# A fused attention and two-layer MLP kernel: two half-bank output accumulators, freer input products, casts on either of two engines, and a re-planned order

## Chip, cores and metric

One NeuronCore of a Trainium2 chip runs the whole program in a single launch. The metric is the device time of that launch in microseconds; the time before is the median of three runs.

## The reference

Attention with a learned position bias, then two MLP layers over its 2304 output rows (4 batches of 576 positions, 8 heads of 64). All results are float32; the weights of the MLP layers come as float64.

```python
scores = q @ k.T / 8 + bias          # bias[i, j, h] = relu(x @ w1 + b1) @ w2, x = log1p|i-j| / log1p(max(i,1))
attn = softmax(scores)
x = concat_heads(attn @ v)           # (2304, 512)
h = x @ w_in                         # 512 -> 2048
x = (s * relu(h)**2 + b) @ w_out     # 2048 -> 512: the first layer
h = x @ w_in2
out = (h - tanh(h)) @ w_out2         # the second layer
```

## The kernel before

**Engines.** PE multiplies, DVE and ACT do the elementwise work and read PSUM, POOL does some subtractions in SBUF, and SP issues every DMA. All products are made from float16 pairs: a value is split into a high half (a cast) and a low half (value minus high half), and a product is high x high, high x low and low x high, three matmuls.

**Order.** Nothing is issued in the order of the code. Each piece of work is a `Task` with its dependencies, a cost for each engine that could do it, a priority, and the buffers that it takes. `Schedule.forward` (L266) plays the program through with these costs and emits each task where it was played, so that every engine's queue is a fixed list in the built program. Buffers are counted by rings (L560): a task that takes a buffer of a ring waits until the users of the oldest one are done. Tables at the top of the file set the plan: `COST` and `XFER` correct the costs by kind of task, `ENGINE` pins single tasks to an engine, `SHIFT` moves the priority of single tasks. A transfer is modelled by the issue time on SP, a bus that takes one transfer after the other, and a delay to landing.

**Stages.** (a) The bias tables, the attention's scales and the first layer's weight conversion; (b) attention in 144 units (`qk` L1003, row minimum L1035, exponential L1045, high half L1055 or L1057, low half on POOL L1064, a transposing DMA L1070, `pv` L1083), and beside it the first layer for the blocks that are complete; (c) behind the last unit the rest of the first layer, while the second layer's weights are loaded (only the attention's buffers have room for them: the `turn` task), converted from float64 by three DVE operations (L1194, L1197, L1200), normed (L1723), split (L582, L585) and combined (L1775); (d) the second layer, whose products are saved from eight to seven by Strassen's scheme (`in_product` L1964, `out_product` L2092).

**The first layer** (`moe1_in` L1474, `moe1_tasks` L1530) works on nine blocks of 256 rows. A block has sixteen input steps of twelve 128x256 matmuls (L1499), two of which fill one PSUM bank `ph`. For each pair ACT takes the relu into `r` (L1512), ACT squares it (L1517), DVE casts it to the high half in `hr` (L1522), and POOL subtracts for the low half (L1526). Rings allow two `ph` banks and two `r` buffers. `hr` exists once: the casts of a block wait until the output steps of the block before are done. Then come four output columns of four steps each (L1568), each step again twelve 128x256 matmuls, gathered over its four steps in `po`. `po` is one PSUM bank in two halves that are used in turn (`po_tile`), but the ring `o` has a single place: the first matmul of a column waits until the column before has been read out by ACT (L1587) or DVE (L1582), two or three instructions by the batch borders in the block. Two lines tie the order on PE:

```python
last = t_poq.get(n - 1, [])[-1:]      # L1540: input steps come after the output steps of block n-1
("h", 2), ("o", 1), ("r", 2),         # L562: rings and their places
```

The second layer also takes a place of ring `o`: the last accumulator of `out_product` is the whole `po` bank.

Of the kernel before, what the change touches and what calls it, by code (L numbers as in the profile page):

```python
# [8 lines left out]
F32 = mybir.dt.float32  # L9
# [21 lines left out]
AHEAD = 5.97  # L31
# [4 lines left out]
    "u.ttr@dve": 0.8262, "f.hi@dve": 1.1781, "x.scale@dve": 1.04, "x.hi@dve": 1.03, "u.hi@dve": 0.9737,  # L36
    "s.in_done@dve": 1.78, "scan.add@dve": 0.73, "f.lambda@dve": 0.884, "s.out_done@dve": 1.2, "u.lo@pool":
    1.03, "f.lo@pool": 0.9595, "bias.lambda@pool": 0.992, "u.qk@pe": 0.885, "u.pv@pe": 0.97, "u.tr@sp": 1.17,
    "x.lambda@sp": 1.07, "q.fn@sp": 1.36, "J.c@dve": 1.13, "J.fn@dve": 1.12, "L.lambda@dve": 1.07,
# [3 lines left out]
    0.857, "v.hi@dve": 1.34, "v.lambda@dve": 0.968, "w.lambda@dve": 0.965, "f.lo@act": 0.95, "f.lo@dve": 0.95,  # L43
    "f.hi@act": 0.99, "f.hi@pool": 0.99, "u.hi@pool": 0.91, "u.ex@dve": 0.8, "u.ex@pool": 0.8, "u.ttr@act":
    0.81, "u.ttr@pool": 0.81,
}
XFER = {
    "bias.fn": (0.927, 0.75), "f.fn": (1.133, 0.55), "k.fn": (1.0815, 0.8), "q.fn": (0.8755, 1.15), "scan.fn":
    (0.9579, 0.8), "u.fn": (1.236, 1.41), "u.tr": (0.9991, 1.54), "v.fn": (1.0712, 1.3), "w.fn": (1.03, 0.87),
    "x.fn": (1.236, 0.55), "x.lambda": (0.721, 3.44), "L.fn": (0.9991, 0.9), "J.fn": (0.721, 0.3), "X.fn":  # L50
    (1.854, 0.4), "o.fn": (0.8858, 0.0),
}
# [331 lines left out]
def tile_kernel(  # L384
# [14 lines left out]
    nc = tc.nc  # L399
# [1074 lines left out]
    def moe1_in(n, o, w, ms, ready, prev_evac, prev, last, t_rlo):  # L1474
# [13 lines left out]
        for fp in range(KF // 2):  # L1488
# [32 lines left out]
            def hi(_, rh=rh, r=r):  # L1521
                nc.vector.tensor_copy(out=rh[:, :, 0, :], in_=r.tile)  # L1522
# [730 lines left out]
```

## Time and profile before

| | |
|---|---|
| median of three runs | 1078.2 us (1075.01 to 1080.54) |
| the profiled execution's own time | 1072.9 us |
| its span, first to last instruction | 1071.1 us |
| PE busy | 962.1 us, 90% of the span |
| DVE busy | 898.9 us, 84% |
| ACT busy | 664.7 us, 62% |
| POOL busy | 350.7 us, 33% |
| last instruction of attention on DVE starts | 572.67 us |

The profile shows one execution. Busy time is the union of an engine's instructions in a stretch; a matmul's row shows its whole passage, some 0.22 to 0.28 us, while matmuls follow each other much closer, so that PE's pace is read from many rows and not from the mean of one. "A <- B" in a list of waits is idle time of A's engine that ended when B was done.

### The profile page before, as it was taken

The numbers are of one execution on the slowest core, as the hardware profiler recorded it, in microseconds if no ns is written. First come the engines' busy times: TensorE is split into PE (matmuls) and PEld (weight loads), VectorE is DVE, ScalarE is ACT, GpSimd is POOL, SyncE is SP. The second block draws the span as 40 slices with busy tenths as digits, with TensorE's granted clock in tenths as the row PEclk, the third lists the DMA queues.
The fourth block names the chain that finished last, engine by engine and source line by source line (L and its number), as shares of the span: only waits on it lengthen the run. The fifth ranks groups of instructions, "written<-read, shape, count | busy, mean of one in ns | idle before, by whom it ended". The sixth has DMA issues, their size and how long they took to land.

```text
span 1071.1 us, 32375 instructions
## 1 busy us (share of the span) xinstructions
PE 962.1 (90%) x13370; PEld 820.5 (77%) x13370; DVE 898.9 (84%) x1914; ACT 664.7 (62%) x1279; POOL 350.7 (33%) x371
## 2 busy tenths in 40 slices
PE   5565658999998899999999898987999999999998
PEld 2222236778787688787888787877999999999998
DVE  6899899767668777786773989889999999999876
ACT  6788879868766576777753575656645543344433
POOL 6034355646456376585762342300000000000000
PEclk9667669999999999999999999999999999999999
DMA  9969987999999999989996705310101100100001
GB/s 340 360 153 250 296 230 149 208 211 255 244 181 234 201 171 199 206 172 194 173 171 167 300 10 173 105 36 16 32 23 41 42 22 31 32 22 22 21 2 41
DMA packets 261444, 153.66 MB, mean 143 GB/s; under 512 B 197680, under 2 KB 229552, under 8 KB 261296
## 3 DMA queue, kind: packets, MB, share of 16 engines
q1 hardware_dynamic: 261296, 151.59, 58.8%
q8 instruction: 104, 1.70, 0.7%
q14 instruction: 44, 0.36, 0.1%
HBM read 84.03 MB, written 20.33 MB: 97 GB/s over the span
## 4 chain that ended last, share of the span: by engine, by line
PE 55%; DVE 21%; DMA 12%; ACT 4%; issue 4%; POOL 3%; SPq 1%; DVEq 0%; ACTq 0%; POOLq 0%
PE acc L2092 13%; PE ph L1499 9%; PE pa L1964 8%; PE po L1568 8%; DMA et<-hl 8%; PE pb L1964 6%; PE sp L1003 3%; DVE w1big L585 3%; DVE sp L1035 2%; PE po L2092 2%; PE xp L1083 2%; POOL hr L692 1%; ACT e L1045 1%; DMA w1big<-in_wout 1%; DMA bi<-btd 1%
## 5 line engine op out<-in xcount | busy, mean ns | idle before, releaser
L1064 POOL TENSOR_TENSOR hl<-e,hl 128x64 f16<-128x64 f32 (+1 forms) x288 | 231.9, 828 | 221.0 <-ACT hl L1057 93.6
L1568 PE MATMUL po<-hr,w1big 128*128 128x256 f16 x1728 | 205.8, 275 | 13.2 <-ACT x L1587 8.6
L1568 PEld LDWEIGHTS <-w1big 128*128 128x128 f16 x1728 | 166.7, 99 | 39.2 <-issue 18.8
L1499 PEld LDWEIGHTS <-w1big 128*128 128x128 f16 x1728 | 165.2, 98 | 26.7 <-issue 8.0
L1964 PEld LDWEIGHTS <-w2big 128*128 128x128 f16 x3024 | 174.1, 98 | 4.2 <-issue 4.2
L2092 PEld LDWEIGHTS <-w1big 128*128 128x128 f16 x3024 | 172.8, 98 | 2.1 <-issue 2.1
L1045 ACT ACTIVATE e<-sp,mx 128x576 f32<-128x576 f32 x144 | 105.7, 734 | 53.7 <-DVE mx L1039 39.2
L1526 POOL TENSOR_TENSOR hr<-r,hr 128x512 f16<-128x512 f32 x72 | 100.4, 1396 | 115.8 <-DVE hr L1522 104.6
L1035 DVE CUSTOM_DVE_ANT_0 sp<-sp,bi 128x576 f32<-128x576 f32 x144 | 109.6, 761 | 31.9 <-PE sp L1003 26.5
L1499 PE MATMUL ph<-xt_own,w1big 128*128 128x256 f16 x960 | 112.5, 273 | 1.0 <-ACT r L1512 0.6
L1003 PE MATMUL sp<-ks,qs 64*128 64x288 f16 (+1 forms) x960 | 82.8, 298 | 13.9 <-ACT e L1045 11.3
L1083 PEld LDWEIGHTS <-et 128*128 128x128 f16 (+1 forms) x1440 | 54.9, 103 | 49.8 <-DMA et<-hl 26.6
L1499 PE MATMUL ph<-w1big 128*128 128x256 f16 x768 | 89.7, 275 | 1.6 <-ACT r L1512 1.2
L1083 PE MATMUL xp<-vp,et 128*128 128x64 f16 (+1 forms) x1440 | 65.5, 198 | 23.5 <-DMA et<-hl 17.8
L1057 ACT ACTIVATE hl<-e 128x576 f16<-128x576 f32 x100 | 67.5, 680 | 24.4 <-DMA et<-hl 21.1
L2092 PE MATMUL acc<-hr,w1big 128*128 128x128 f16 x1296 | 80.2, 219 | 1.8 <-DVE hr L585 1.2
L1003 PEld LDWEIGHTS <-qs 64*128 64x128 f16 (+1 forms) x960 | 46.3, 99 | 43.0 <-issue 32.8
L2092 PE MATMUL acc<-w2big,w1big 128*128 128x128 f16 x1296 | 79.1, 219 | 0.0
L1964 PE MATMUL pa<-w1big,w2big 128*128 128x128 f16 x960 | 61.2, 221 | 4.0 <-ACT w1big L1983 4.0
L1512 ACT ACTIVATE r<-ph 128x512 f32<-128x512 f32 x72 | 42.6, 592 | 31.0 <-PE ph L1499 22.4
L1522 DVE CAST hr<-r 128x512 f16<-128x512 f32 x72 | 42.2, 588 | 17.6 <-ACT r L1517 16.0
L1517 ACT ACTIVATE r<-r,sq 128x512 f32<-128x512 f32 x72 | 51.8, 720 | 1.5
(225 smaller groups left out, 1686.1 us busy)
## 6 DMA issues: line engine op xcount, KB each, us to landing
bi<-btd SPq DMA_DIRECT2D x64, 288.0 KB, 4.1
w1big<-in_wout SPq DMA_DIRECT2D x12, 1024.0 KB, 5.8
btd<-et SPq DMA_DIRECT2D x36, 295.5 KB, 4.4
w1big<-in_win SPq DMA_DIRECT2D x8, 1024.0 KB, 8.0
w2big<-in_win SPq DMA_DIRECT2D x8, 1024.0 KB, 12.8
x2d<-x SPq DMA_DIRECT2D x36, 128.0 KB, 2.2
w1big<-x2d SPq DMA_DIRECT2D x36, 128.0 KB, 2.4
outT<-xt_own SPq DMA_DIRECT2D x18, 256.0 KB, 2.2
```

The costliest lines, as they stand in the source:

```text
L1003: nc.tensor.matmul(out=out, lhsT=qs.tile[64 * h:64 * h + 64, sq, p * r:p * r + r], rhs=ks.tile[64 * h:64 * h + 64, sk, half * HS:(half + 1 ...
L1035: nc.vector.tensor_tensor_reduce(out=st, in0=st, in1=bi.tile.rearrange("p (a b) -> p a b", a=2), scale=-1.0 / KAP, scalar=3.0e38, op0=ALU. ...
L1045: nc.scalar.activation(out=put(e, row_tile("e")).rearrange("p (a b) -> p a b", a=2), in_=sp.tile[:, :, 0:HS], func=AF.Exp, scale=-1.0, bia ...
L1057: nc.scalar.activation(out=h[:, 0:S], in_=e.tile, func=AF.Copy)
L1064: (nc.gpsimd if eng == POOL else nc.vector).tensor_tensor(out=hl.tile[:, o:o + m], in0=e.tile[:, c:c + m], in1=hl.tile[:, c:c + m], op=ALU ...
L1083: nc.tensor.matmul(out=xp[r0:r0 + r, o:o + 64], lhsT=et.tile[:, n, r0:r0 + r], rhs=vp.tile[:, 0, n % 5, 64 * h:64 * h + 64], start=n == 0, ...
L1499: nc.tensor.matmul(out=ph.tile[:, fi, :], lhsT=win_ap(1, sw, m, f), rhs=xa(sx, m), start=m == 0 and j == 0, stop=m == KM - 1 and j == 2,)
L1517: nc.scalar.activation(out=r.tile, in_=r.tile, func=AF.Square, scale=sq[:, fp // 4:fp // 4 + 1])
L1526: (nc.gpsimd if e == POOL else nc.vector).tensor_tensor(out=rh[:, :, 1, :], in0=r.tile, in1=rh[:, :, 0, :], op=ALU.subtract)
L1568: nc.tensor.matmul(out=po.tile[:, :NB1], lhsT=wout_ap(1, sw, f, c), rhs=rhl[f // 8][:, f % 8, sr, :], start=f == 0 and j == 0, stop=f == K ...
L1964: nc.tensor.matmul(out=bank.tile[:, f * HT:(f + 1) * HT], lhsT=w[:, sw, m, f * 128:(f + 1) * 128], rhs=xs[:, sx, m], start=p in (1, 2, 5) ...
L2092: nc.tensor.matmul(out=bank.tile[:, o + c * HT:o + (c + 1) * HT], lhsT=w[:, sw, f, c * 128:(c + 1) * 128], rhs=g[:, sx, f], start=new and ...
```

## The change

1. Ring `o` has two places, so a column may start in the other half of the `po` bank while the half before is read out. Where the second layer uses `po` as a whole it takes both places (`more`).
2. The input steps of block n come after the input steps of the block before, no longer after its output steps.
3. The high-half cast in the first layer may run on ACT as well as on DVE. The table pins the casts of blocks 0, 1, 3, 4, 5, 7 and 8 to ACT, those of block 2 to DVE, and leaves block 6 open; the program has 57 on ACT and 15 on DVE.
4. The small tile `nm` has nine buffers in place of one.
5. The planner's model: SP is held longer by an issue when the modelled bus has a backlog (`BACK`), and COST, XFER, HOP, AHEAD, ENGINE and SHIFT have new numbers. With them the order of all engines is new. The instructions are the same apart from the engine that runs them: against before, DVE loses 57 casts L1522 and 32 scaled copies L580 and gains 14 casts L1055, 7 read-outs L1582 and 7 relus L692; ACT has the converse.

```diff
-    HOP = dict(pe=0.33, act=0.07, dve=0.16, pool=0.41, turn=0.0)
+    HOP = dict(pe=0.25, act=-0.04, dve=0.1, pool=0.61, turn=0.0)
+    BACK, BACK_MIN, BACK_HOLD = 0.5, 1.6, 1.1
...
-                free[eng] = at + cost[0]
+                hold = cost[0]
+                if eng == "sp" and hold > self.BACK_HOLD and bus - at > self.BACK_MIN:
+                    hold += self.BACK * (bus - at - self.BACK_MIN)
+                free[eng] = at + hold
...
-        ("h", 2), ("o", 1), ("r", 2), ("xt", 4), ("x2", 2), ("xf", 2), ("xh", 2), ("sum", 4),
+        ("h", 2), ("o", 2), ("r", 2), ("xt", 4), ("x2", 2), ("xf", 2), ("xh", 2), ("sum", 4),
...
-            nm = c2_t[n, o, "m"] = sm.tile([128, 1], F32, tag="nm", name="nm", bufs=1)
+            nm = c2_t[n, o, "m"] = sm.tile([128, 1], F32, tag="nm", name="nm", bufs=9)
...
-            def hi(_, rh=rh, r=r):
-                nc.vector.tensor_copy(out=rh[:, :, 0, :], in_=r.tile)
-            th = sc.add({DVE: 0.07 + 0.6e-3 * 2 * w}, hi, [ts] + prev, ready - 400, [], [r])
+            def hi(e, rh=rh, r=r):
+                if e == DVE:
+                    nc.vector.tensor_copy(out=rh[:, :, 0, :], in_=r.tile)
+                else:
+                    nc.scalar.activation(out=rh[:, :, 0, :], in_=r.tile, func=AF.Copy)
+            th = sc.add({DVE: 0.07 + 0.6e-3 * 2 * w, ACT: 0.17 + 0.9e-3 * 2 * w}, hi, [ts] + prev, ready - 400, [], [r])
...
-        last = t_poq.get(n - 1, [])[-1:]
+        last = list(t_in1)
...
             st[j // 2] = inst("o" if j == 6 else "q")
+            st["more"] = [inst("o")] if j == 6 else []
...
+        more = st["more"] if j == 6 else []
...
-            {PE: 1.345}, mm, t_gl[k, p] + t_wp[1, s, p] + last_pe, base, [bank] if new else [], [bank],
+            {PE: 1.345}, mm, t_gl[k, p] + t_wp[1, s, p] + last_pe, base, [bank] + more if new else [], [bank] + more,
...
+    "s1.lambda": "dve", "f0.hi": "act", "f1.hi": "act", "bias4.lambda": "dve", "k1.hi": "act", "f2.hi": "dve",
```

**DVE, right behind its last attention instruction.** Before: the last low half of attention rows (L1144), the scales of the next block (L1458 and on), and then casts (L1522) among the three conversion operations of the second layer's weights (L1194, L1197, L1200; 1024 is a quarter of a weight pair).

```order
L1194 TENSOR_SCALAR w2big<-w2big 128x1024
L1197 SCALAR_TENSOR_TENSOR w2big<-w2big 128x1024
L1522 CAST hr<-r 128x2x256
L1200 SCALAR_TENSOR_TENSOR w2big<-w2big 128x1024
L1194 TENSOR_SCALAR w2big<-w2big 128x1024
L1522 CAST hr<-r 128x2x256
L1197 SCALAR_TENSOR_TENSOR w2big<-w2big 128x1024
```

In the changed kernel, at the same place (lines are ten further down; L1533 is the cast):

```order
L1533 CAST hr<-r 128x2x256 x3
L1204 TENSOR_SCALAR w2big<-w2big 128x1024
L1207 SCALAR_TENSOR_TENSOR w2big<-w2big 128x1024
L1210 SCALAR_TENSOR_TENSOR w2big<-w2big 128x1024
L1204 TENSOR_SCALAR w2big<-w2big 128x1024
L1207 SCALAR_TENSOR_TENSOR w2big<-w2big 128x1024
L1210 SCALAR_TENSOR_TENSOR w2big<-w2big 128x1024
```

No cast stands on DVE behind these three, up to the end of the program; before, 24 stand behind the last attention instruction, now 4. The read-outs of `po` (L1582) in this part, five instructions before, are gone from DVE too.

**ACT, from the read-outs of block 6 to the first relus behind them.** Before: the read-out of a column (L1587), squares of the second layer's weights (L1723), scaled copies of those weights (L582), and only then the next block's relu (L1512) and square (L1517).

```order
L1587 ACTIVATE x_10429<-po,bcol,esc 128x128 x2
L1723 ACTIVATE junk,ss_w_137<-w2big 128x512 x2
L582 ACTIVATE w2big<-w2big,w_0_c 128x1024 x4
L1512 ACTIVATE r<-ph 128x512
L582 ACTIVATE w2big<-w2big,w_0_c 128x1024
L1517 ACTIVATE r<-r,sq_9378 128x512
```

In the changed kernel (L1600 is the read-out, L1736 the squares, L1535 the cast, L592 the scaled copy, L1522 and L1527 relu and square):

```order
L1736 ACTIVATE junk,ss_w_137<-w2big 128x512 x4
L1535 ACTIVATE hr<-r 128x2x256 x2
L1600 ACTIVATE x_10597<-po,bcol,esc 128x128 x2
L1522 ACTIVATE r<-ph 128x512
L1527 ACTIVATE r<-r,sq_9484 128x512
L1522 ACTIVATE r<-ph 128x512
L1535 ACTIVATE hr<-r 128x2x256
L1527 ACTIVATE r<-r,sq_9484 128x512
L1535 ACTIVATE hr<-r 128x2x256
L592 ACTIVATE w2big<-w2big,w_0_c 128x1024 x4
```

The casts of the next block now run on ACT, and two of them stand ahead of the last read-out of the block before: its relus and squares had been made by then.

## Rows read from the trace of the kernel before

**Rows 1.** Windows: stretch, length, busy us (instructions) of PE, PEld, DVE, ACT, POOL, clock, DMA

```profile
0.00:160.00 160.00, 94.21 (x787) 42.45 (x788) 142.42 (x274) 122.85 (x238) 64.61 (x53) 0.73 0.92 272
160.00:577.00 417.00, 397.02 (x5385) 324.79 (x5384) 307.37 (x812) 293.76 (x644) 245.41 (x294) 0.99 0.97 195
577.00:760.00 183.00, 163.75 (x1716) 146.33 (x1715) 163.58 (x245) 112.35 (x196) 40.73 (x24) 0.97 0.32 111
760.00:1072.00 312.00, 307.08 (x5490) 306.91 (x5487) 285.52 (x585) 135.72 (x202) 0.00 (x0) 1.00 0.09 28
```

**Rows 2.** What PE waited for, 577 to 760 us: total us, times, longest

```profile
PE po L1568 <- ACT x L1587: 6.5, 7, 1.1
PE pa L1964 <- ACT w1big L1983: 4.0, 1, 4.0
PE po L1568 <- POOL hr L1526: 2.7, 2, 1.6
PE psum L657 <- DVE cols L1819: 1.9, 1, 1.9
PE ph L1499 <- ACT r L1512: 1.2, 2, 0.9
...
PE ph L1499 <- DVE na L1458: 0.3, 1, 0.3
```

**Rows 3.** What PE waited for, 160 to 577 us

```profile
PE xp L1083 <- DMA et<-hl: 8.9, 15, 1.0
...
PE po L1568 <- ACT x L1587: 2.1, 3, 1.0
PE po L1568 <- DVE x L1582: 1.6, 3, 0.6
...
PE ph L1499 <- ACT et L582: 0.4, 1, 0.4
```

**Rows 4.** Groups of instructions, 577 to 760 us: busy us, mean ns | idle before, releasers

```profile
L1499 PE MATMUL ph<-xt_own,w1big 128*128 128x256 f16 x192 | 21.1, 273 | 0.0
...
L1517 ACT ACTIVATE r<-r,sq 128x512 f32<-128x512 f32 x24 | 17.3, 719 | 0.6
...
L1512 ACT ACTIVATE r<-ph 128x512 f32<-128x512 f32 x24 | 14.3, 596 | 21.9 <-PE ph L1499 15.5 <-POOL hr L1526 6.3
L1522 DVE CAST hr<-r 128x512 f16<-128x512 f32 x24 | 13.7, 570 | 8.5 <-ACT r L1517 7.4 <-issue 1.1
...
L1587 ACT ACTIVATE x<-po,bcol,esc 128x128 f32<-128x128 f32 (+1 forms) x23 | 8.8, 438 | 11.1 <-PE po L1568 11.1
...
L1582 DVE TENSOR_SCALAR x<-po,esc,bcol 128x128 f32<-128x128 f32 (+1 forms) x5 | 1.6, 378 | 4.4 <-PE po L1568 4.4
```

**Rows 5.** Timeline of DVE: start us, length us, instruction, count, [idle before]

```profile
572.67 0.43 DVE L1144 TENSOR_TENSOR xh<-xf,xh 128x256 f16<-128x256 f32 x1
...
587.12 0.43 DVE L1522 CAST hr<-r 128x512 f16<-128x512 f32 x1 [2.19 <-ACT r L1517]
587.49 0.69 DVE L1194 TENSOR_SCALAR w2big<-w2big 128x1024 uint32<-128x1024 uint32 x1
...
637.54 1.38 DVE L1522 CAST hr<-r 128x512 f16<-128x512 f32 x1
```

**Rows 6.** What ACT waited for, 577 to 760 us

```profile
ACT r L1512 <- PE ph L1499: 15.5, 13, 2.1
...
ACT junk L1723 <- DVE w2big L1200: 10.7, 8, 3.0
ACT w1big L582 <- DVE w2big L1775: 8.8, 6, 3.7
...
ACT w1big L582 <- DVE w_c L457: 0.2, 1, 0.2
```

**Rows 7.** The page, a group on ACT: the cast of attention's high half

```profile
L1057 ACT ACTIVATE hl<-e 128x576 f16<-128x576 f32 x100 | 67.5, 680 | 24.4 <-DMA et<-hl 21.1
```

More of the change, by code (lines that the diff above doesn't have):

```diff
@@ L30 @@
 WI0, WI1, WO0, WO1 = 27.23, 74.31, 71.56, 137.63
-AHEAD = 5.97
+AHEAD = 5.67
 COST = {
@@ L35 @@
     "w.square@act": 1.07, "k.hi@act": 1.15, "s.lambda@act": 1.09, "q.hi@act": 1.2, "v.hi@act": 1.14,
-    "u.ttr@dve": 0.8262, "f.hi@dve": 1.1781, "x.scale@dve": 1.04, "x.hi@dve": 1.03, "u.hi@dve": 0.9737,
+    "u.ttr@dve": 0.9486, "f.hi@dve": 1.5351, "x.scale@dve": 1.04, "x.hi@dve": 1.03, "u.hi@dve": 0.9737,
     "s.in_done@dve": 1.78, "scan.add@dve": 0.73, "f.lambda@dve": 0.884, "s.out_done@dve": 1.2, "u.lo@pool":
-    1.03, "f.lo@pool": 0.9595, "bias.lambda@pool": 0.992, "u.qk@pe": 0.885, "u.pv@pe": 0.97, "u.tr@sp": 1.17,
-    "x.lambda@sp": 1.07, "q.fn@sp": 1.36, "J.c@dve": 1.13, "J.fn@dve": 1.12, "L.lambda@dve": 1.07,
+    1.03, "f.lo@pool": 1.01, "bias.lambda@pool": 0.992, "u.qk@pe": 0.885, "u.pv@pe": 0.97, "u.tr@sp": 1.04,
+    "x.lambda@sp": 1.083, "q.fn@sp": 1.36, "J.c@dve": 1.13, "J.fn@dve": 1.12, "L.lambda@dve": 1.07,
     "L.square@act": 0.919, "P.wsum@dve": 0.942, "X.scales@dve": 0.83, "X.sums@dve": 1.21, "X.xsum@dve": 1.19,
@@ L42 @@
     1.22, "k.hi@dve": 1.24, "k.lambda@dve": 0.939, "q.hi@dve": 1.06, "s.lambda@dve": 0.952, "scan.lambda@dve":
-    0.857, "v.hi@dve": 1.34, "v.lambda@dve": 0.968, "w.lambda@dve": 0.965, "f.lo@act": 0.95, "f.lo@dve": 0.95,
-    "f.hi@act": 0.99, "f.hi@pool": 0.99, "u.hi@pool": 0.91, "u.ex@dve": 0.8, "u.ex@pool": 0.8, "u.ttr@act":
-    0.81, "u.ttr@pool": 0.81,
+    0.857, "v.hi@dve": 1.34, "v.lambda@dve": 0.968, "w.lambda@dve": 0.965, "f.hi@act": 1.29, "f.hi@pool": 1.29,
+    "u.hi@pool": 0.91, "u.ex@dve": 0.8, "u.ex@pool": 0.8, "u.ttr@act": 0.93, "u.ttr@pool": 0.93,
 }
 XFER = {
[L48 to L51, printed above, removed]
+    "bias.fn": (0.83121, 1.21), "f.fn": (1.5759, 0.69), "k.fn": (1.11343, 1.19), "q.fn": (1.09901, 1.27),
+    "scan.fn": (0.84254, 1.47), "u.fn": (1.26793, 2.96), "u.tr": (1.0609, 1.68), "v.fn": (1.01146, 1.73),
+    "w.fn": (0.95584, 1.49), "x.fn": (1.236, 1.0), "x.lambda": (0.85181, 4.09), "L.fn": (0.91258, 2.06), "J.fn":
+    (0.34608, 0.98), "X.fn": (1.60577, 0.87), "o.fn": (0.8858, 0.45), ".fn": (0.82091, 0.86),
 }
@@ L56 @@
 ENGINE = {
[5 rows of a table removed]
+    "s1.lambda": "dve", "f0.hi": "act", "f1.hi": "act", "bias4.lambda": "dve", "k1.hi": "act", "f2.hi": "dve",
+    "v2.hi": "dve", "f3.hi": "act", "k2.hi": "dve", "f0.out": "act", "u14.hi": "act", "u12.hi": "act", "f4.hi":
+    "act", "f4.out": "dve", "u7.hi": "act", "bias4.out": "act", "f7.hi": "act", "u6.hi": "dve", "u5.hi": "act",
[3 rows of a table added]
+    "act", "bias0.out": "act", "I13.lambda": "act", "f6.out": "act", "I11.lambda": "act", "I2.lambda": "act",
+    "I3.lambda": "dve", "I16.lambda": "act", "k3.hi": "act", "I5.lambda": "act", "X7.lambda": "act",
+    "I4.lambda": "act", "I6.lambda": "act", "bias3.out": "act", "X6.lambda": "act", "X3.lambda": "act",
 }
@@ L247, in add @@
                 if isinstance(c, tuple):
-                    k, d = XFER.get(kind, (1.03, 0.8))
-                    t.opts[e] = (c[0] * COST.get(kind + "@" + e, 1.0), c[1] * k, d)
+                    k, d = XFER.get(kind, (1.03, 1.25))
+                    t.opts[e] = (c[0] * 0.98 * COST.get(kind + "@" + e, 1.0), c[1] * k, d)
                 else:
@@ L2114, in psum_add @@
                     out=out(), in0=half(bank.tile, h), scalar=osc, in1=add(), op0=ALU.mult, op1=ALU.add
-                ), [t] + deps, pr, takes, list(uses) + [bank], share=0.0,
+                ), [t] + deps, pr, takes, list(uses) + [bank] + more, share=0.0,
             )
```

215 rows, old and new, of tables (ENGINE, SHIFT) are left out of this document.

## The prediction

> **What bounds the kernel now.** I read the windows first, by stage [rows 1]. From 160 us on PE is the engine that sets the end: it is busy for 397.02 of 417 us while attention runs, for 163.75 of 183 us in the transition behind attention, and for 307.08 of 312 us in the second layer, which is a plain wall of matmuls until the last few microseconds. The reader is to see that PE's work is the same before and after the change, so that behind 160 us only its idle time can be won or added: 20.0 us in the second stretch, 19.2 us in the third, next to nothing in the fourth. The third row has a second message. DVE is busy for 163.58 of 183 us there and hardly rests once the second layer's weights have landed, so it comes close to setting the pace itself; ACT has 112.35 us and room. In the first 160 us PE is not the limit; DVE is, with 142.42 us.
>
> Then I read what PE waited for, in the two stretches apart. In the transition nine waits add to 19.0 us, all but a trace of its idle time [rows 2]. The largest is the read-out of `po`: 6.5 us in seven waits, so 0.93 us at each change of column. The low half on POOL (2.7 us) and the relu (1.2 us) belong to the first layer's own chain. The rest, 4.0 and 1.9 us and three smaller ones of 2.4 us in all, is the second layer starting: its operands come off DVE and ACT late. While attention runs, nine waits add to 19.3 us [rows 3]; 8.9 us of that is for the transposing DMAs, and 2.1 and 1.6 us is for the read-out of `po` again.
>
> **The accumulators in halves.** A column of the output takes four steps. The row of the input steps gives PE's pace: 192 matmuls of 128x256 in 21.1 us [rows 4], 0.110 us each, 1.32 us for a step of twelve and 5.3 us for a column. Its read-out is two instructions of 0.438 us on ACT [rows 4]. With two places a column waits for the read-out of the column before the last, which then has 5.3 us of cover; only where ACT is later than that does the wait come back. The most that can go is the sum of both stretches, 10.2 us [rows 2, 3]; the least is nothing. In the transition there is little else for PE to do at a change of column, so I take 5.8 of the 6.5 us. Beside attention PE's queue is a mix and the new order has its own places for each wait, so I take half of 3.7 us, 1.8 us. Together 7.6 us.
>
> A matmul then writes one half of a bank while ACT reads the other, which no row of before shows. The Trainium skill speaks against that (PSUM — Partial Sum Buffer, Summary: rules for kernel authors: while a matmul runs, read a different bank, and guard by bank). It adds (PSUM bank collisions raise a hardware error) that the hardware neither arbitrates nor stalls, so by the page the overlap costs no time, and by its guard the 7.6 us would not be had at all.
>
> **The casts on ACT.** Behind attention's last instruction DVE made 24 casts of 0.570 us on average [rows 4], a plain one taking 0.43 us and one that ran into POOL 1.38 us [rows 5]. Four of them stay. So DVE loses 20 x 0.570 = 11.4 us, and with the five read-outs of 1.6 us [rows 4] 13.0 us, from the stretch where it is nearly full. ACT gains 20 casts. No row shows this cast on ACT; the nearest is attention's, 0.680 us for 576 columns [rows 7], which scales to 0.60 us for 512; the relu of the same size takes 0.596 us [rows 4]. That is 12.1 us more, and about 2 us of read-outs, on 112.35 us of 183. For a pair of input steps, 2.64 us of PE, ACT then spends 0.596 + 0.719 + 0.60 = 1.92 us: it keeps up, and the detour over DVE is gone. POOL's low half no longer waits for a cast that stands behind a conversion of one to two microseconds.
>
> What this is worth on PE lies between nothing and the waits that hang on it: 2.7 us on POOL, and 4.0 + 1.9 + 2.4 us at the start of the second layer, 11.0 us [rows 2]. I take a third, 3.6 us, and the reason is the next part.
>
> **Input products ahead, and the new order.** The casts of a block still wait for the output steps of the block before, since `hr` exists once; so two `r` and two `ph`, four pairs, eight steps, can run ahead, and the new order of PE does so before blocks 1, 3, 7 and, in part, 8. I counted PE's steps behind the last attention product: before, 48 input and 50 output steps; now 41 and 48. Nine steps, 9 x 1.32 = 11.9 us, have moved ahead of attention's end. That work is neither gained nor lost, but it pushes attention's end back by up to 11.9 us unless it fills idle time there. The loads of the second layer's weights cannot start before attention has given its memory up: 14.8 us lie between DVE's last attention instruction and its first conversion (572.67 to 587.49 us, [rows 5]). So DVE's chain starts up to 11.9 us later and is 13.0 us shorter, and the second layer's operands come only slightly earlier. With 20.0 us of idle time beside attention some of the nine steps will find a gap. Hence a third of 11.0 us, not all of it.
>
> The first 160 us get a new order, with seven relus moved onto DVE. DVE has 17.6 us of idle time there [rows 1]; half of it, 8.8 us, is my bound for either sign, and I take zero. The new order of SP's queue can move the 8.9 us for the transposes [rows 3] to nothing or double it; zero again. The nine `nm` buffers remove a wait that no row shows, and the second layer's claim on both halves is the whole bank as before: zero, hidden behind products whose operands are there.
>
> **Sum.** 7.6 + 3.6 = 11.2 us. The profiled execution took 1072.9 us, 1.8 us beyond its span, and becomes 1061.7 us. It lies 5.3 us under the median of the runs, so against the median the forecast is 1078.2 - 11.2 = 1067.0 us.
>
> **The rivals.** *Given back.* PE reaches the second layer earlier, and DVE's chain, 11.9 us later and 13.0 us shorter, lets it in only 1.1 us earlier than before: 1077 us. If only the overlap in one bank fails, by a guard or by the two accesses holding each other up, the 3.6 us remain: 1074.6 us. For it speaks DVE at 163.58 of 183 us; against it, that DVE spent some of that stretch on work for later blocks.
>
> *Attention takes the steps for nothing.* All nine steps fall into its 20.0 us of idle time, attention ends when it did, DVE's chain is a full 13.0 us earlier and all of 11.0 us goes: 7.6 + 11.0 = 18.6 us, 1059.6 us. With the bound of the first stretch, 8.8 us more, 1050.8 us. For it: most of attention's waits are for transfers, which other work can fill. Against it: a step of 1.32 us is longer than the longest single wait listed, 1.0 us.
>
> *ACT's queue holds the first layer up, and the kernel is slower.* In the transition ACT stands still for the second layer's weights, 10.7 us before the squares and 8.8 us before scaled copies, up to 3.7 us at a time [rows 6]. Before, the cast was on another engine; now relu, square and cast all stand behind such a wait. If two of them meet, 7 us pass, more than the two pairs (5.3 us) that PE has in hand, and PE stops. If the whole 19.5 us falls on PE and 7.6 us is won, the time is 1078.2 + 11.9 = 1090.1 us. The Trainium skill has the same leaning (ScalarE: Activation LUTs, Rules for kernel authors: a relu, multiply or add belongs on VectorE); the rows agree in so far as 0.60 us stands against 0.43 us. Against the rival: relu and square were in that queue already, and only 1.2 us of PE's waits came of it.
>
> **How the numbers follow.** The forecast gets 0.40, given back 0.24, attention for nothing 0.20, ACT's queue 0.16. A difference of 0.5%, 5.4 us, is about what a measurement of this kernel can tell: under 1072.8 us counts as faster, over 1083.6 us as slower. Faster is 0.40 + 0.20 = 0.60, the same 0.24, slower 0.16. The range runs from 1050 us, the far end of the second rival with the first stretch, to 1083 us, given back with some loss to the transfers; the third rival lies outside. The forecast's own range is 1060 to 1073 us.
>
> **What would show it.** Right: PE's wait for the read-out of `po` falls from 10.2 us to under 3 us over the span; the row of DVE behind attention is some 13 us shorter and ACT's longer; PE's idle time in the transition falls to about 10 us, and attention ends at 575 to 585 us. Given back: PE's wait for the read-out is gone, but waits of the second layer's first products for DVE and ACT have grown by as much. ACT's queue: `ph` or `po` waits for relu, cast or POOL by several microseconds at a time. I would be wrong if the first 160 us moved by over 9 us, or if the waits for transposes doubled.

## The result, and the profile after

The changed kernel takes 1086.2 us (median of six runs, 1084.5 to 1087.3) beside 1075.6 us for the kernel before on the same chips: ratio 1.0092, 95% interval 1.0067 to 1.0117, so it is slower by 0.9%. The forecast was 1067 us, and the range ended at 1083 us; it was reckoned down from 1078.2 us, so 2.6 us of the distance is the kernel before, which these runs put lower.

The list of PE's waits in the changed kernel, from 584 us, where PE has done the work that it had done at 577 us before, to 773.4 us (before: 760 us). Line numbers are ten to thirteen further down: L1581 is the output step, L1600 and L1595 its read-out on ACT and DVE, L1509 the input step, L1522 the relu.

```profile
PE po L1581 <- ACT x L1600: 8.5, 9, 1.2
PE pb L1977 <- DVE w2big L2003: 3.2, 1, 3.2
PE pa L1977 <- ACT w2big L1996: 2.5, 1, 2.5
PE po L1581 <- POOL hr L1539: 2.3, 2, 1.3
PE ph L1509 <- ACT r L1522: 1.6, 1, 1.6
PE psum L667 <- ACT r L1522: 1.4, 1, 1.4
```

And from 161.6 to 584 us:

```profile
PE xp L1093 <- DMA et<-hl: 7.4, 7, 1.9
...
PE po L1581 <- DVE x L1595: 3.2, 5, 1.9
...
PE po L1581 <- ACT x L1600: 2.3, 3, 0.9
```

The wait that was to go, 10.2 us before [rows 2, 3], is the largest of the transition still and 14.0 us in all. Where it stands now shows in the timeline of PE, changed kernel, the columns of one block (start, length, instruction, count, idle before):

```profile
614.87 6.71 PE L1581 MATMUL po<-hr,w1big 128*128 128x256 f16 x60
622.47 5.40 PE L1581 MATMUL po<-hr,w1big 128*128 128x256 f16 x48 [0.90 <-ACT x L1600]
628.77 5.40 PE L1581 MATMUL po<-hr,w1big 128*128 128x256 f16 x48 [0.90 <-ACT x L1600]
635.07 4.09 PE L1581 MATMUL po<-hr,w1big 128*128 128x256 f16 x36 [0.90 <-ACT x L1600]
```

A column is 48 matmuls. The first stretch has 60 and the last 36: PE does a whole column and the first step of the next, twelve matmuls, and then stands still for 0.90 us. The wait has moved from the first step to the second. The timeline of ACT shows why it has not become shorter:

```profile
621.62 0.81 ACT L1600 ACTIVATE x<-po,bcol,esc 128x128 f32<-128x128 f32 x2 [3.60 <-PE po L1581]
```

The column's own last step was over at about 620.2 us (twelve matmuls, 1.3 us, before the pause), and ACT was idle for 3.60 us; but the read-out starts only at 621.62 us, when the first step of the next column is done. `po` is one tile, and in these rows the waits that the program was built with keep everything that touches it in the order in which it was issued, whichever half it touches. The planner counts two places, so it issues the read-out behind the next column's first step; the read-out then waits for that step, and the second step waits for the read-out. The Trainium skill (PSUM — Partial Sum Buffer, PSUM bank collisions raise a hardware error) asks for this guard: PSUM is to be guarded by bank and quadrant, not by address. The trace agrees in so far as the waits of this program treat the two halves of the bank as one place; whether they go by bank or by tile, no run here tells apart.

The windows after, for stretches of equal work:

```profile
0.00:161.60 161.60, 100.85 (x827) 43.52 (x827) 140.77 (x275) 127.05 (x248) 67.42 (x55) 0.78 0.94 275
161.60:584.00 422.40, 399.17 (x5248) 325.87 (x5244) 300.34 (x803) 285.71 (x633) 244.49 (x291) 0.98 0.93 188
584.00:773.40 189.40, 166.90 (x1831) 149.19 (x1829) 154.34 (x228) 120.94 (x221) 38.81 (x26) 0.97 0.33 111
773.40:1084.60 311.20, 306.49 (x5476) 306.17 (x5473) 273.89 (x548) 161.10 (x241) 0.00 (x0) 1.00 0.09 28
```

Against [rows 1] the second layer is the same to a microsecond, DVE has 9.2 us less in the transition and ACT 8.6 us more, and the transition is 6.4 us longer all the same (8.5 us by the yardstick below, whose marks lie further apart). The end of attention has moved by more than was thought; on DVE, the last instruction of attention (before at 572.67 us, [rows 5]) and the first conversion of the second layer's weights (before at 587.49 us) are now

```profile
593.59 0.42 DVE L1154 TENSOR_TENSOR xh<-xf,xh 128x256 f16<-128x256 f32 x1
...
606.43 0.69 DVE L1204 TENSOR_SCALAR w2big<-w2big 128x1024 uint32<-128x1024 uint32 x1
```

**A yardstick for the experiments.** Orders differ, so I mark time by PE's work: every matmul of the trace is counted at its steady pace (0.109 us for a 128x256 one, and so on by shape), 876 us in all. After 40 us of work the first stage is over, after 400 attention is nearly over, after 600 the second layer is running. Times between the marks, one profiled execution each, in us:

| kernel | 40 to 400 | 400 to 600 |
|---|---|---|
| before | 397.7 | 229.7 |
| changed | 401.8 | 238.2 |
| changed, one place | 410.8 | 237.9 |
| changed, banks | 400.9 | 230.2 |
| changed, casts on DVE | 400.3 | 241.9 |
| changed, input after output | 415.4 | 248.6 |
| before, two halves | 409.0 | 232.4 |
| before, banks | 402.9 | 229.0 |
| before, casts on ACT | 404.2 | 235.6 |
| before, banks and casts | 396.9 | 228.0 |
| before, input ahead | 400.3 | 250.0 |
| sums later | 401.8 | 222.6 |
| best | 401.5 | 225.8 |

From 600 to 860 every kernel takes 259.9 to 260.4 us. Seven of these kernels have the order of before up to attention's end; their first column runs from 396.9 to 404.2 us, with PE's waits for the transposing DMAs between 7.3 and 11.8 us. So the 4.1 us between the first two rows there cannot be told from the spread; what the change did is read from the 8.5 us of the second column, one execution each.

### The profile page after: what moved, and what is told of

It is laid out like the page before. It is cut to its first block, busy times and chain, and to the rows that moved or that the text cites. A ratio compares the mean times of both kernels' runs of the same rounds, so it can differ in the third digit from the quotient of the medians.

```text
span 1084.6 us, 32339 instructions
## 1 busy us (share of the span) xinstructions
PE 973.4 (90%) x13370; PEld 824.8 (76%) x13370; DVE 869.3 (80%) x1853; ACT 694.8 (64%) x1340; POOL 350.7 (32%) x371
## 5 line engine op out<-in xcount | busy, mean ns | idle before, releaser
L1074 POOL TENSOR_TENSOR hl<-e,hl 128x64 f16<-128x64 f32 (+1 forms) x288 | 235.6, 841 | 232.9 <-ACT hl L1067 119.6
L1581 PE MATMUL po<-hr,w1big 128*128 128x256 f16 x1728 | 202.1, 273 | 16.3 <-ACT x L1600 10.8
L1581 PEld LDWEIGHTS <-w1big 128*128 128x128 f16 x1728 | 166.2, 98 | 41.3 <-issue 22.3
L1509 PEld LDWEIGHTS <-w1big 128*128 128x128 f16 x1728 | 167.1, 99 | 32.1 <-issue 11.5
L1055 ACT ACTIVATE e<-sp,mx 128x576 f32<-128x576 f32 x144 | 105.8, 735 | 81.7 <-DVE mx L1049 61.0
L1509 PE MATMUL ph<-xt_own,w1big 128*128 128x256 f16 x960 | 115.3, 278 | 0.7 <-ACT r L1522 0.7
L1013 PE MATMUL sp<-ks,qs 64*128 64x288 f16 (+1 forms) x960 | 83.1, 300 | 14.3 <-ACT e L1055 14.3
L1509 PE MATMUL ph<-w1big 128*128 128x256 f16 x768 | 89.8, 274 | 3.1 <-ACT r L1522 2.5
L1067 ACT ACTIVATE hl<-e 128x576 f16<-128x576 f32 x86 | 57.9, 678 | 11.9 <-DMA et<-hl 10.9
L1522 ACT ACTIVATE r<-ph 128x512 f32<-128x512 f32 x72 | 42.3, 588 | 28.1 <-PE ph L1509 21.2
L1527 ACT ACTIVATE r<-r,sq 128x512 f32<-128x512 f32 x72 | 51.5, 718 | 1.1
L1977 PE MATMUL pb<-w1big,w2big 128*128 128x128 f16 x720 | 45.6, 224 | 3.8 <-DVE w2big L2003 3.2
```

The costliest lines, as they stand in the source:

```text
L1013: nc.tensor.matmul(out=out, lhsT=qs.tile[64 * h:64 * h + 64, sq, p * r:p * r + r], rhs=ks.tile[64 * h:64 * h + 64, sk, half * HS:(half + 1 ...
L1055: nc.scalar.activation(out=put(e, row_tile("e")).rearrange("p (a b) -> p a b", a=2), in_=sp.tile[:, :, 0:HS], func=AF.Exp, scale=-1.0, bia ...
L1067: nc.scalar.activation(out=h[:, 0:S], in_=e.tile, func=AF.Copy)
L1074: (nc.gpsimd if eng == POOL else nc.vector).tensor_tensor(out=hl.tile[:, o:o + m], in0=e.tile[:, c:c + m], in1=hl.tile[:, c:c + m], op=ALU ...
L1509: nc.tensor.matmul(out=ph.tile[:, fi, :], lhsT=win_ap(1, sw, m, f), rhs=xa(sx, m), start=m == 0 and j == 0, stop=m == KM - 1 and j == 2,)
L1527: nc.scalar.activation(out=r.tile, in_=r.tile, func=AF.Square, scale=sq[:, fp // 4:fp // 4 + 1])
```

## Experiments on the changed kernel

In all experiments the planner makes its plan as before, and the tasks are issued in that order but for the edit; an "edge" from A to B holds B back until A has been issued.

**One place (one_place).** The read-out of column i is issued ahead of the first step of column i + 1.

```diff
+    return list(zip(outs, cols[1:]))      # edges: read-out of a column -> first step of the next
```

> Changed kernel, order kept, but each read-out of a column is issued ahead of the first step of the next column, as a ring of one place would have it. Guard theory (both halves of the bank are guarded as one, so the wait only moved from a column's first step to its second and grew): PE's waits for the read-out of po fall from 14.0 us to about 10 us, and the time by 2 to 4 us, to 1082 to 1084 us. Order theory (the loss comes from the new order, not from the accumulators) and ACT theory: within 1.5 us of the changed kernel, 1085 to 1088 us.

Measured: 1093.0 us, ratio to before 1.0181 (1.0155 to 1.0207). Every expectation missed. The waits for the read-out grew to 24.3 us, and the loss lies beside attention (410.8 against 401.8 us). The changed order was planned for two places, and here a step issued ahead of the read-out covers a part of the wait; that the read-outs stand late in ACT's and DVE's queues because the plan sees no hurry is my reading, not shown. So the two places are worth something in the order that was made for them. That does not make them a gain over before.

**Columns in different banks (banks).** Behind attention PSUM banks are free. Even columns of blocks 6 to 8 go into one of these; the order is unchanged.

```diff
-                        put(po, make())
+                        put(po, p2["g"].tile([128, 512], F32, tag="g", name="po") if "g" in p2 and c % 2 == 0 else make())
```

> Changed kernel, order the same, but from the turn on (blocks 6, 7 and 8) the even columns are gathered in a PSUM bank of their own, so that two columns share no bank. Guard theory: PE's waits for the read-out behind 592 us fall from 8.5 us to under 1.5 us, the gaps of 1.17 us at each column change go, and the time falls by 6 to 8 us, to about 1079 us. Rival, the second layer's operands set the end of the transition: the gaps go as well, but the waits of the first products of the second layer for DVE and ACT grow by as much, and the time stays within 2 us of the changed kernel.

Measured: 1078.4 us, ratio 1.0041 (1.0022 to 1.0059); the profiled span falls from 1084.6 to 1076.5 us. The same block in PE's timeline:

```profile
613.76 21.12 PE L1581 MATMUL po<-hr,w1big 128*128 128x256 f16 x192
```

All 192 matmuls run through in 21.12 us; in the changed kernel they took from 614.87 to 639.16 us, 24.3 us. The waits in this stretch (583.8 to 764.3 us) begin with

```profile
PE pa L1977 <- ACT w2big L1996: 4.8, 1, 4.8
PE po L1581 <- POOL hr L1539: 4.1, 3, 1.8
PE pb L1977 <- DVE w2big L2003: 2.4, 1, 2.4
```

and no read-out is among them. 8.0 us of the 8.5 us come back (238.2 to 230.2). Against the changed kernel the guard theory holds and "given back" does not, though the waits for ACT and POOL grew by 4.1 us. Against the kernel before it is the other way: the read-outs that cost 6.5 us there are gone from this list, but its waits add to 18.3 us beside 19.0, and the stretch takes 230.2 us beside 229.7. A second place that works does not make this order faster than before either. What is left against before, 0.4% in the medians, lies in no one stretch of these executions.

**Casts back on DVE (casts_dve).** The 16 casts of blocks 7 and 8.

```diff
-                if e == DVE:
+                if e == DVE or n >= 7:
```

> Changed kernel, order the same, but the 16 casts of blocks 7 and 8 run on DVE in place of ACT, at their places in the order. ACT theory (relu, square, cast and read-out all stand in ACT's queue and hold up DVE's small scales and the second layer): DVE's wait for the scales of a block (3.9 us) goes, the time falls by 4 to 9 us, to 1077 to 1082 us. Rival (DVE sets the pace in the transition): DVE gets 16 x 0.57 = 9.1 us more, the second layer's first products come later, and the time rises by 3 to 9 us, to 1089 to 1095 us. Guard theory alone: within 2 us.

Measured: 1087.1 us, ratio 1.0134 (1.0106 to 1.0161), against 1.0092 (1.0067 to 1.0117) with the casts on ACT; the intervals touch. In the trace the transition is 3.7 us longer, and PE's wait for POOL's low half 5.4 us in place of 2.3. By the plain medians (1087.1 against 1086.2 us) this is within the 2 us of the guard theory alone; by the ratios it is some 4 us, where the rival began. So the casts on ACT are no loss in this order, by the trace a gain, and they are not what made the kernel slower.

**Input steps behind output steps again (in_after_out).**

```diff
+        # edge: last output step of block n - 1 -> first input step of block n
+        e.append((next(d for d in out[3].deps if d.key.endswith(".mm")), mm[0]))
```

> Changed kernel, order kept but for one rule put back: the input steps of a block come behind the last output step of the block before. Run-ahead theory (the nine steps ahead of attention's end push the transition back): the last attention product ends about 10 us sooner than 592 us, the second layer's weights are loaded that much sooner, and the time falls by 3 to 9 us, to 1077 to 1083 us. Rival (the steps ahead fill PE's gaps): PE stands still at three or four changes of block for the chain of relu, square, cast and low half, 2 to 3 us each, and the time rises by 3 to 9 us. Guard theory alone: within 2 us.

Measured: 1110.9 us, ratio 1.0341 (1.0315 to 1.0368): much slower, beside attention (415.4 us) and in the transition (248.6 us). The rival had the sign, but the rise is about 25 us where it had 3 to 9. The changed order rests on the steps that run ahead. Without them the read-out waits are 15.3 us in the transition, one of them 7.7 us: a late read-out now finds PE with nothing in hand.

## Experiments on the kernel before

**Two halves alone (b_two_halves).** Order of before; only the read-out moves behind the next column's first step, as the change has it.

```diff
+    return [(cols[i + 1], outs[i]) for i in range(36) if i % 4 < 3]   # edges: first step of the next column -> read-out
```

> Kernel before with its own order, and only the accumulators' part of the change: within a block the read-out of a column is issued behind the first step of the next column, which goes into the other half of the bank. Step of the prediction (halves overlap): PE's waits for the read-out, 10.2 us, fall to about 3 us and the time by up to 7 us, to 1066 us. Guard theory (the wait moves to the second step, and the read-out now starts 1.3 us later): the waits stay at 10 us or grow, 27 column changes by 0 to 0.25 us, and the time is the same to 7 us above, 1073 to 1080 us.

Measured: 1086.9 us, ratio 1.0101 (1.0068 to 1.0134). This one edit makes the kernel before as slow as the whole change. PE's waits for the read-out, up to 589.4 us and behind it:

```profile
PE po L1568 <- ACT x L1587: 6.1, 8, 1.1
...
PE po L1568 <- DVE x L1582: 4.8, 7, 0.8
```

```profile
PE po L1568 <- ACT x L1587: 11.6, 9, 3.1
```

22.5 us in 24 waits, in place of 10.2 us in 13; the 12.3 us more are close to the slowdown of 11.6 us, which is above the 7 us that the guard theory allowed. By the yardstick most of it lies beside attention (409.0 us; 232.4 against 229.7 in the transition), where the whole change lost most of its time in the transition: two halves cost time in both orders, but in different places. Two things are seen to make it so. Where PE had other work between two columns (beside attention, and in block 8, where second-layer products stood between the columns), the read-out used to be over when the next column began; now it cannot start before that. A column of block 8 on PE, before, and then with two halves, twelve matmuls and a wait:

```profile
708.37 5.40 PE L1568 MATMUL po<-hr,w1big 128*128 128x256 f16 x48
```

```profile
722.77 1.47 PE L1568 MATMUL po<-hr,w1big 128*128 128x256 f16 x12
725.38 4.09 PE L1568 MATMUL po<-hr,w1big 128*128 128x256 f16 x36 [1.14 <-ACT x L1587]
```

And a read-out that starts late meets what is next in ACT's queue: ACT waited 17.5 us for `po` in this transition, 11.1 us before [rows 4], and what stands behind it waits as well. In the timeline of ACT a square stands ahead of a read-out that could have started with it, and the pause of PE behind was 1.47 us in place of 0.90:

```profile
628.65 0.60 ACT L1723 ACTIVATE junk<-w2big 128x512 f32<-128x512 f32 x1 [1.69 <-DVE w2big L1200]
629.19 0.19 ACT L1723 ACTIVATION_READ_ACCUMULATOR junk<-w2big 128x1 f32 x1
629.28 0.79 ACT L1587 ACTIVATE x<-po,bcol,esc 128x128 f32<-128x128 f32 x2
```

**Banks, casts, and both (b_banks, b_casts_act, b_banks_casts).** Order of before.

```diff
-                        put(po, make())
+                        put(po, p2["g"].tile([128, 512], F32, tag="g", name="po") if "g" in p2 and (n < 8 and c % 2 == 0 or n == 8 and c == 0) else make())
...
-                nc.vector.tensor_copy(out=rh[:, :, 0, :], in_=r.tile)
+                nc.vector.tensor_copy(out=rh[:, :, 0, :], in_=r.tile) if n < 7 else nc.scalar.activation(out=rh[:, :, 0, :], in_=r.tile, func=AF.Copy)
```

> Kernel before with its own order, but from the turn on the even columns of blocks 6 and 7 and the first column of block 8 are gathered in a PSUM bank of their own. Guard theory with PE as the bound: the waits for the read-out in the transition, 6.5 us, fall to 1 us and the time by 4 to 6 us, to 1067 to 1069 us, under both kernels. Given back: the first products of the second layer wait for DVE and ACT by as much more, and the time stays within 2 us of before, 1071 to 1075 us.

> Kernel before with its own order, but the casts of blocks 7 and 8 run on ACT in place of DVE. Step of the prediction: DVE loses 16 to 19 casts of 0.57 us, some 10 us, POOL's low half is not late any more and the second layer starts up to 3.6 us sooner: 1070 to 1073 us. ACT theory (a cast behind a squares or scaled copy that waits holds the relu of the next pair up): PE's waits for POOL's low half and for the relu grow, and the time rises by 2 to 8 us, to 1075 to 1081 us.

> Kernel before with its own order and both: even columns in a bank of their own behind attention, and the casts of blocks 7 and 8 on ACT. If the second layer's operands take the gain of the banks back because DVE is full, the casts make room and the two together give more than their sum: 1064 to 1068 us. If the two are independent: the sum of the two single runs. If ACT's queue is the limit: no better than the banks alone.

Measured: banks 1076.4 us, ratio 1.0004 (0.9985 to 1.0023); casts 1078.3 us, 1.0017 (0.9985 to 1.0050); both 1074.3 us, 0.9992 (0.9966 to 1.0018). None differs from before. With banks the read-out wait in the transition fell from 6.5 to 0.5 us, and the list now begins:

```profile
PE pa L1964 <- ACT w1big L1983: 4.0, 1, 4.0
PE ph L1499 <- ACT r L1512: 3.9, 3, 2.6
PE po L1568 <- POOL hr L1526: 2.7, 2, 1.6
PE psum L657 <- DVE s2w L1737: 2.7, 1, 2.7
PE psum L657 <- DVE cols L1819: 2.3, 1, 2.3
```

That is "given back": PE, now early, waits 2.7 us more for the relu than before (3.9 against 1.2 us) and 2.7 us for a small sum of two matmuls that did not wait, with work behind them. With the casts alone one profiled wait for the relu was 5.7 us, the rival of ACT's queue at work; that execution was also 7 us above the median of its kernel.

**Input ahead (b_ahead).** Order of before, and the first eight input steps of blocks 7 and 8 go ahead of the last output column of the block before.

```diff
+        for k, t in enumerate(steps_in[n][:8]):
+            rank[t.seq] = at - 0.5 + 0.02 * k      # at: the place of that column's first step
...
```

> Kernel before with its own order, but only the input steps run ahead: the first eight input steps of blocks 7 and 8 go ahead of the last output column of the block before, with the first two relus and squares. Step of the prediction (work moved, neither gained nor lost): within 2 us of before, 1073 to 1077 us. Filler theory (steps in hand cover PE's waits, as in the changed order, where taking them back cost 2.5%): 2 to 5 us faster. Chain theory (the moved steps leave PE nothing to do while the first casts, low halves and the third relu of the block run): PE's waits for the relu grow by 2 to 3 us at each of the two blocks, 1077 to 1081 us.

Measured: 1096.1 us, ratio 1.0183 (1.0151 to 1.0216), four times the worst that was expected. PE's list from 580.9 to 783 us begins with the relu:

```profile
PE ph L1499 <- ACT r L1512: 13.8, 2, 7.7
```

and ACT's timeline shows the third relu of block 7, and what the fourth stood behind:

```profile
638.78 0.60 ACT L1512 ACTIVATE r<-ph 128x512 f32<-128x512 f32 x1 [11.04 <-POOL hr L1526]
640.61 5.30 ACT L582 ACTIVATE w2big<-w2big,w_c 128x1024 f16<-128x1024 f32 x5 [1.23 <-DVE w_c L457]
646.70 4.27 ACT L582 ACTIVATE w2big<-w2big,w_c 128x1024 f16<-128x1024 f32 x4 [0.79 <-DVE w2big L1775]
650.88 0.71 ACT L1517 ACTIVATE r<-r,sq 128x512 f32<-128x512 f32 x1
651.49 0.57 ACT L1512 ACTIVATE r<-ph 128x512 f32<-128x512 f32 x1
```

Nine scaled copies of the second layer's weights. In the order of before the first relus of the block stand between them; those had now been issued ahead, so the copies follow each other. And they came late, because the sum that gives their scale takes a place of ring `h` on PE and had itself waited 3.3 us for the third relu. That one had waited for POOL's low half: the steps ahead had filled both `r` buffers, whose casts wait for the output of the block before, so there was no place for a third. This is close to the third rival's mechanism, in an order that was not made for steps ahead.

## A version that beats both

**Sums later, best (b_sums_later, b_best).** The kernel with banks and casts; three small sums stand two steps later on PE. The second adds three moves on DVE and ACT.

```diff
+    for k, n, i in (("L0.mm", 6, 15), ("L1.mm", 8, 1), ("X1.mm", 8, 13)):
...
+        extra.append((steps_out[n][i], t))         # edge: output step i of block n -> the sum
...
+    rank[2683] = rank[2678] + 0.5                  # best: a sum of weights ahead of two low halves, DVE
...
+        rank[t.seq] = max(rank[t.seq], rank[relu[8][1 + k // 2].seq] + 0.5 + 0.01 * k)   # best: four squares behind relus
...
+    rank[relu[7][2].seq] = rank[p[-1].seq] - 0.5   # best: a relu ahead of a scaled copy
```

> The kernel before with banks of their own and the casts of blocks 7 and 8 on ACT, and three small sums of the second layer (two matmuls each) moved later on PE, behind two to five steps that stood after them. Order theory (the gain of the banks is given back because PE, now earlier, meets sums whose inputs are not ready, and stands still with work behind them): the waits of these sums, 2.7, 1.3 and 2.3 us, fall to under 1 us in all, and the time falls by 3 to 6 us against the same kernel without this edit, to 1069 to 1072 us, under both kernels. Rival (the second layer's operands are late whatever PE does): the waits reappear at the second layer's first products, 1073 to 1076 us.

> The kernel of the sums moved later, with three more moves in the order: on DVE the first sum of the last weights goes ahead of two low halves, on ACT four squares of the second layer's last weights go behind the second and third relu of block 8, and one relu of block 7 a scaled copy forward. Order theory (what is left in the transition are waits behind instructions of ACT and DVE that could stand later): PE's wait for ACT before the second layer's products falls from 4.6 us to about 2 us, its waits for the relu from 5.1 us to about 3 us, and the time falls by 2 to 5 us against the kernel of the sums, to 1068 to 1071 us, 0.4 to 0.7% under before. Rival (the weights' chain on DVE sets the start of the second layer): the waits move to other operands and the time stays at 1072 to 1075 us.

Measured: sums later 1073.3 us, ratio 0.9981 (0.9955 to 1.0008); best 1070.1 us, ratio 0.9954 (0.9933 to 0.9974), which is faster than before by 0.5% and than the changed kernel by 1.4% (0.9954 / 1.0092). With the sums later, their waits (6.3 us in the kernel with banks and casts) are gone and the transition takes 222.6 us in the profiled execution, 228.0 without the edit; but a part comes back at the relu and the second layer's first products, and the median, 1073.3 us beside 1074.3, differs neither from that kernel's nor from before. The three further moves did not do what was expected of them; PE's list for the best kernel, 581.4 to 760 us:

```profile
PE ph L1499 <- ACT r L1512: 5.9, 6, 2.5
PE pa L1964 <- ACT w1big L1983: 4.4, 1, 4.4
```

The two waits they aimed at were 5.1 and 4.6 us without them. The intervals of the two kernels overlap, so what the three moves add is open; that the whole set beats before is not.

## Why the prediction was wrong

**The step that failed first** is this one: "With two places a column waits for the read-out of the column before the last, which then has 5.3 us of cover." The two places were in the plan's counting of rings, not in the waits of the program. The read-out of a column and the first step of the next are ordered one behind the other, and so the wait went from the first step to the second. I took 7.6 us of gain, with nothing as the least; the waits grew by 3.8 us. The least was wrong too: an overlap that fails does not leave the old state, since the order had been changed to suit it. The two-halves run prices that at 1.0% by itself, and the banks run returns 8.0 of the 8.5 us in the transition.

**A second step failed behind it:** that a read-out wait taken from PE is time won ("I take 5.8 of the 6.5 us"). In the banks runs of both orders this wait is gone from the transition, or 0.5 us, and the time is 0.4% above before in the one and the same as before in the other; other waits took its place. So "given back" came true in its effect, in both orders, though by the relu, POOL's low half, small sums and the second layer's operands together and not by DVE's chain alone; the forecast would have failed with a second place that worked, too.

**"If only the overlap in one bank fails, by a guard"** was the rival that named the mechanism, at 1074.6 us. It kept the waits as they were, still counted 3.6 us for the casts, and was 11.6 us too low against the measured 1086.2.

**The casts, 3.6 us:** near the mark in the traces of this order, where the casts of blocks 7 and 8 on ACT save 3.7 us of transition; the medians of those two kernels are 0.9 us apart and their intervals touch, so the size stays open. A cast on ACT takes 0.623 us, estimated at 0.60; these groups are from 584 to 773.4 us of the changed kernel:

```profile
L1535 ACT ACTIVATE hr<-r 128x512 f16<-128x512 f32 x17 | 10.5, 623 | 0.2
...
L1533 DVE CAST hr<-r 128x512 f16<-128x512 f32 x7 | 3.9, 551 | 14.1 <-ACT r L1527 14.1
```

For the single instruction DVE is the faster one; for the kernel it was no loss to use the engine with room. The Trainium skill (ScalarE: Activation LUTs, Rules for kernel authors) gives relu, max, min, add and multiply to VectorE; a cast is not in its list, but 551 against 623 ns points the same way. In the order of before the same move is worth nothing that can be measured.

**The steps ahead, "neither gained nor lost":** wrong as a price of a part by itself. Put into the order of before they cost 1.8%, taken out of the new order 2.5%. Attention's end on DVE moved by 20.9 us, where 11.9 us was my bound; the nine steps account for 11.9 us at most, and no run took the rest apart.

**Right:** the first 160 us (40 us of work are done at 163.8 us before, at 164.4 us now), the transposes (7.4 us against 8.9), and the second layer as a wall. **The slower rival** had the sign but not the cause: the changed kernel waits 3.0 us for relus in the transition, and giving the casts back to DVE does not make it faster.

**Still open:** whether two engines on the two halves of one bank would disturb each other. A version without the guard was not tried, because nothing would keep the two apart. The 0.4% that the banks leave is not located, nor are the parts additive: two halves alone cost as much as the whole change, and each part depends on the order around it.

## What to carry to other kernels

A second place for a buffer is worth something only if the program's waits see two buffers: look at which instruction the wait stands on after the change, and look past the first one, since a planner that believes in the second place issues the reader later and makes a false place cost more than none. A wait taken from an in-order engine gives time only if the instructions next in its queue are ready earlier too; here the banks gave nothing by themselves, and only with the casts, three sums of two matmuls and three further moves did the kernel come out 0.5% faster. Price a part of a change in the order in which it will run: input steps ahead were worth 2.5% in one order and cost 1.8% in another.

## What the runs showed of the hardware

The pause at a change of column is the same, 0.90 us, whether it stands before the first step (before) or behind it (changed): a column takes 6.30 us either way, as the starts of PE's rows show; those of before are

```profile
604.06 5.40 PE L1568 MATMUL po<-hr,w1big 128*128 128x256 f16 x48 [0.90 <-ACT x L1587]
610.36 5.40 PE L1568 MATMUL po<-hr,w1big 128*128 128x256 f16 x48 [0.90 <-ACT x L1587]
```

The pause costs a little more than is listed: the 192 matmuls of a block take 24.3 us with three pauses and 21.1 us without (banks), so 1.06 us each.

A long pause of PE seems to cost more than its length. In the run with input ahead PE stood still for 3.3 us before 639 us and for 7.7 us before 652 us; the windows around these pauses (the figure behind POOL's count is the granted clock, as a share of 2.4 GHz, the other level being 1.2 GHz) are

```profile
630.00:640.00 10.00, 6.54 (x59) 5.60 (x57) 1.69 (x7) 0.60 (x1) 2.28 (x2) 1.00 0.04 15
640.00:650.00 10.00, 4.33 (x24) 3.09 (x24) 9.57 (x18) 8.60 (x9) 0.00 (x0) 0.73 0.00 0
650.00:660.00 10.00, 7.83 (x59) 6.34 (x59) 9.59 (x11) 6.79 (x10) 5.98 (x3) 0.76 0.00 0
```

The waits listed for that transition add to 33.3 us against 19.0 before, 14.3 us more, while the same work took 20.3 us longer. The mean granted clock of the transition is 0.92 there (580.9 to 783 us) against 0.97 before; it is the likely remainder, which no run took apart.
